# An attention and mixture-of-experts kernel: laying the attention's usual arm behind the general arm

## The chip, the core and the metric

The kernel runs on one core of one Trainium2 chip. A core has five engines that run their own instruction streams: PE (TensorE, matrix products), DVE (VectorE), ACT (ScalarE), POOL (GpSimd) and SP (SyncE, which here only issues transfers). They wait for each other by semaphores, and 16 DMA engines move data between the chip's memory and the core. The metric is the device time of one execution in microseconds (us); a time without further words is the median of several executions.

## What is computed

A windowed attention with four sink positions, and on its output a mixture of experts with one expert for each token. Cut to what matters:

```python
# attention: batch 4, heads 8, sequence 768, head size 64; n_sink = 4, window = 128
scores = q @ k.T / sqrt(64)
keep = (key < n_sink) | ((0 <= query - key) & (query - key < window))
a = softmax(where(keep, scores, -1e9))
x = (a @ v)                      # laid out as 3072 tokens x 512
# experts: 8, hidden size 1024
e = argmax(x @ w_gate); g = softmax(x @ w_gate)[e]
out = g * (relu(x @ w1[e]) @ w2[e])
```

n_sink and window are inputs of the kernel, so the kernel finds them only when it runs.

## The kernel before

The program has three stretches. In the first, to about 4 us, constants are made, the first pieces of q, k and v are loaded, and `flag()` (L711) compares n_sink and window with the usual values 4 and 128 and leaves the answer, `usual`, in a register of every engine.

The second is the attention. `tc.If(usual == 1)` (L756) has two arms. The usual arm, `fast_attention` (L448), works on tiles of 128 queries for a pair of heads, 96 steps s for 16 pairs k, and its order on each engine is written out by hand. A step holds the scores of tile s (`scores`, L509, three products of split operands f_kh, f_kl, f_qh, f_ql), the merge of masks and the maximum on DVE (L521, L523, L528), the exponentials on ACT (`exps`, L535), transposes on PE (L543), and the weighted sum with v (L570, L572). Between them ACT, DVE and POOL split the next pair's k and q into a high and a low part (`prep`: f_kh L475, f_qh L481, f_kl L478, f_ql L484), from the buffers kd and qd that SP loads (L414, L415). The loads of pairs 0 and 1 are issued ahead of the If, those of pair 2 and later, of the sinks (vs, L446) and of the gate's weights within the arm. The usual arm ends with the turn of the first tokens of expert 0 (x-rows gathered by POOL at L133, transposed at L146, split at L161 on ACT and L164 on DVE into exh and exl). The general arm, `general_attention` (L311) with the loads and splits of expert 0's weights, covers every other n_sink and window. With these inputs it isn't run. It has loops, and its instructions on every engine lie in the program's memory between the usual arm and what follows the If.

So the instructions of every engine lie in this order: the start, the compare-and-branch of the If, the usual arm, an unconditional branch past the general arm, the general arm, and the third stretch. The profile records both branches under L756.

The third stretch is the mixture of experts. It begins with the early chunk (256 tokens of expert 0, products at L911 and L933) beside the gate's last tokens (x_tp transposes at L146, gt_xT copies at L199), and with the first splits of expert 1's weights (whi on ACT at L91, wlo on DVE at L94, from wraw). Then come eight experts, each with a switch (recorded under L1114) that jumps to a body for the number of tokens the expert got.

## Time and profile before

| what | value |
|---|---|
| median of 3 executions | 628.39 us (626.49 to 630.0) |
| the profiled execution: its own time | 630.58 us |
| its span, first to last instruction | 628.9 us |
| outside the span | 1.7 us |
| mean granted share of the TensorE clock | 0.96 |
| busy: PE, PE weight loads, DVE, ACT, POOL | 89%, 77%, 49%, 44%, 35% |

Times in the profile count from the start of the span. A row of the timeline has the start, the duration, the engine, the line of the kernel, the operation, and in brackets how long the engine had been idle before it and what ended that; "issue" is idle time in which the engine waited for nothing that the profile shows. PEld is the weight load of PE; a q behind an engine's name is its sequencer, the part that reads instructions and takes branches.

### The profile page before, as it was taken

The page shows a single profiled execution, that of the slowest core. Times are in us where ns is not written, and L with a number is a line of the kernel's source. Part 1 is how long each engine was busy: PE and PEld are TensorE (multiplying, and loading weights), DVE is VectorE, ACT ScalarE, POOL GpSimd, SP SyncE. Part 2 cuts the span into 40 slices and gives each one's busy share as a digit, 9 for nine tenths or more (in the row PEclk, how much of TensorE's full clock was granted, in tenths as well). Part 3 has the DMA queues.
Part 4 walks back from the last instruction along what each step waited for, and adds up shares of the span by engine and source line. Part 5 has one row for each costly group of instructions (what it writes and reads, how often), then busy time and mean ns, then how long its engine had stood idle before and what let it go on. Part 6 is the DMA issues. An engine that isn't in the chain of part 4 may idle for free. (4 is left out here: it accounts for less than half of the span.)

```text
span 628.9 us, 11023 instructions
## 1 busy us (share of the span) xinstructions
PE 560.3 (89%) x3734; PEld 481.8 (77%) x3734; DVE 306.0 (49%) x699; ACT 274.0 (44%) x700; POOL 219.2 (35%) x384
## 2 busy tenths in 40 slices
PE   3999999799989998797979999999999978699982
PEld 2778887588767877686969988888998867598852
DVE  4676638655776476553414333453353626253300
ACT  4567665465655553522313232443343534243320
POOL 5568657573767455003014010302312111141010
PEclk9999999989998999798989999999999988899988
DMA  8234420942094106453416142463532737262010
GB/s 241 83 112 170 131 78 2 246 156 79 32 227 168 60 2 158 131 151 107 134 41 200 35 127 61 158 203 100 192 110 66 256 103 252 97 190 98 2 44 17
DMA packets 36016, 75.79 MB, mean 121 GB/s; under 512 B 4353, under 2 KB 17153, under 8 KB 35844
## 3 DMA queue, kind: packets, MB, share of 16 engines
q1 hardware_dynamic: 31204, 59.25, 31.1%
q0 software_dynamic: 4640, 14.70, 7.1%
q8 instruction: 53, 0.87, 0.6%
q14 instruction: 119, 0.97, 0.5%
HBM read 61.34 MB, written 12.99 MB: 118 GB/s over the span
## 5 line engine op out<-in xcount | busy, mean ns | idle before, releaser
L911 PE MATMUL hp<-xh,whi 128*128 128x256 f32 (+4 forms) x320 | 99.0, 309 | 16.2 <-issue 14.8
L915 ACT ACTIVATE hh<-hp 128x256 fp32r<-128x256 f32 (+4 forms) x88 | 36.0, 410 | 162.9 <-PE hp L911 162.7
L918 DVE SCALAR_TENSOR_TENSOR hl<-hp,hh 128x256 fp32r<-128x256 f32 (+4 forms) x88 | 39.7, 453 | 135.3 <-ACT hh L915 83.9
L953 POOL DMA_INDIRECT moe_out<-rows,idxs x26 | 25.4, 978 | 217.1 <-DVE rows L945 118.9
L911 PE MATMUL hp<-xh,wlo 128*128 128x256 f32 (+4 forms) x320 | 98.7, 308 | 0.0
L911 PE MATMUL hp<-xl,whi 128*128 128x256 f32 (+4 forms) x320 | 98.6, 308 | 0.0
L94 DVE TENSOR_TENSOR wlo<-wraw,whi 128x1024 fp32r<-128x1024 f32 x56 | 68.5, 1229 | 27.4 <-ACT whi L91 27.2
L911 PEld LDWEIGHTS hp<-xh,whi 128*128 128x128 f32 x320 | 64.0, 200 | 22.5 <-issue 18.7
L933 PE MATMUL yps<-whi,hh 128*128 128x512 f32 x192 | 79.3, 413 | 1.4 <-ACT hh L915 1.4
L933 PE MATMUL yps<-whi,hl 128*128 128x512 f32 x192 | 76.8, 400 | 0.0
L933 PE MATMUL yps<-wlo,hh 128*128 128x512 f32 x192 | 76.4, 398 | 0.0
L91 ACT CAST whi<-wraw 128x1024 fp32r<-128x1024 f32 (+1 forms) x72 | 68.3, 955 | 15.3 <-DMA wraw<-wcat 12.8
L535 ACT ACTIVATE f_sq<-f_sp,f_nm 128x132 f32<-128x132 f32 (+1 forms) x192 | 61.1, 374 | 27.5 <-DVE f_nm L528 27.5
L570 PE MATMUL f_po<-vt,f_pl 128*128 128x130 f32 x320 | 69.4, 298 | 0.0
L911 PEld LDWEIGHTS hp<-xl,whi 128*128 128x128 f32 x320 | 63.9, 200 | 2.5
L911 PEld LDWEIGHTS hp<-xh,wlo 128*128 128x128 f32 x320 | 63.9, 200 | 0.0
L572 PE MATMUL f_po<-vt,f_pu 128*128 128x130 f32 x320 | 63.1, 279 | 0.0
L543 PE MATMUL f_tp<-ident,f_sq 128*128 128x128 f32 x192 | 43.2, 300 | 20.6 <-ACT f_sq L535 18.4
L133 POOL DMA_INDIRECT rows<-xrow,idxg x30 | 31.8, 1061 | 80.3 <-DVE hl L918 35.6
L553 POOL TENSOR_SCALAR_AFFINE_SELECT f_pl<-f_pu 128x256 f32<-128x256 f32 x80 | 33.0, 413 | 73.9 <-ACT f_pu L547 66.6
L484 DVE SCALAR_TENSOR_TENSOR f_ql<-qd,f_qh 128x384 fp32r<-128x384 f32 x32 | 34.7, 1084 | 47.6 <-ACT f_qh L481 47.4
L570 PEld LDWEIGHTS f_po<-vt,f_pl 128*128 128x128 f32 x320 | 49.5, 194 | 7.3 <-issue 0.7
(180 smaller groups left out, 1089.5 us busy)
## 6 DMA issues: line engine op xcount, KB each, us to landing
wraw<-wcat SPq DMA_DIRECT2D x64, 512.0 KB, 4.1
xrow<-rows SPq DMA_DIRECT2D x8, 769.5 KB, 7.9
vt<-v SPq DMA_DIRECT2D x16, 384.0 KB, 4.0
kd<-kT SPq DMA_DIRECT2D x15, 396.0 KB, 5.7
qd<-qT SPq DMA_DIRECT2D x15, 384.0 KB, 9.2
rows<-xrow,idxg POOLq DMA_INDIRECT x30
moe_out<-rows,idxs POOLq DMA_INDIRECT x26
kd<-kT SPq DMA_DIRECT2D x2, 198.0 KB, 3.6
```

The source lines that it names most:

```text
L91: nc.scalar.copy(out=whi[e % 2][:, j, c], in_=wraw(e, j)[:, c])
L94: engine.tensor_tensor(out=wlo[e % 2][:, j, c], in0=wraw(e, j)[:, c], in1=whi[e % 2][:, j, c].bitcast(F32), op=ALU.subtract)
L484: V.scalar_tensor_tensor(out=ql[:, QZ[z]], in0=qd[:, QZ[z]], scalar=D ** -0.5, in1=qh[:, QZ[z]].bitcast(F32), op0=ALU.mult, op1=ALU.subtract)
L535: nc.scalar.activation(out=sqs[k][:, i, h, :n], in_=sps[u][:, h, :n], func=AF.Exp, bias=nm[:, h:h + 1], scale=1.0)
L543: nc.tensor.transpose(out=tvs[u][:, h], in_=sqs[k][:, i, h, :P], identity=ident)
L553: nc.gpsimd.affine_select(out=pl, in_=pu, pattern=[[0, 2], [1, P]], compare_op=ALU.is_ge, fill=0.0, base=0, channel_multiplier=-1)
L570: nc.tensor.matmul(out=two, lhsT=pl[:, h], rhs=twice(t), start=(i == 0 and h == 0), stop=False, skip_group_check=True)
L572: nc.tensor.matmul(out=two, lhsT=pu[:, h], rhs=twice(t - 1), start=False, stop=False, skip_group_check=True)
L911: nc.tensor.matmul(out=hp[:, :N], lhsT=l, rhs=r[:, c, :N], start=k == 0, stop=k == 3 * NK - 1)
L915: nc.scalar.activation(out=hh[:, :N], in_=hp[:, :N], func=AF.Relu)
L918: V.scalar_tensor_tensor(out=hl[:, :N], in0=hp[:, :N], scalar=0.0, in1=hh[:, :N].bitcast(F32), op0=ALU.max, op1=ALU.subtract)
L933: nc.tensor.matmul(out=y[:self.M[i]], lhsT=l[:, sl], rhs=r, start=(j == 0 and k == 0), stop=(j == NF - 1 and k == 2))
```

## The change

The If is told which of its two blocks is to lie directly behind the compare-and-branch: with `preferred_fallthrough_block=False` it is the Else block, the general arm. The usual arm lies behind the general one. Each engine now reaches the usual arm by a taken branch, and at the usual arm's end it runs on into the third stretch. No operation, no wait and no buffer is another one.

```diff
@@ -753,7 +753,7 @@
             load_qk(1, bufs)
             sink_blocks()
         usual = flag()
-        with tc.If(usual == 1) as br:
+        with tc.If(usual == 1, preferred_fallthrough_block=False) as br:
             fast_attention(bufs, vs)
         with br.Else():
             nc.sync.dma_start(out=wg, in_=w_gate)
```

## Rows read from the trace of the kernel before

**Rows 1.** The page: the span, and the busy time of each engine over it (us, share, instructions).
```profile
span 628.9 us, 11023 instructions
PE 560.3 (89%) x3734; PEld 481.8 (77%) x3734; DVE 306.0 (49%) x699; ACT 274.0 (44%) x700; POOL 219.2 (35%) x384
```

**Rows 2.** The timeline of PE, ACT and DVE around the end of the usual arm (start us, duration us, engine, line, operation, idle before and its releaser).
```profile
252.97 0.65 PE L146 MATMUL f_tp<-ident,rows 128*128 128x128 f32 x4 [0.81 <-DMA rows<-xrow,eidx]
253.66 0.59 ACT L161 CAST exh<-f_tp 128x512 fp32r<-128x512 f32 x1 [0.88 <-PE f_tp L146]
254.28 0.69 DVE L164 TENSOR_TENSOR exl<-f_tp,exh 128x512 fp32r<-128x512 f32 x1 [0.78 <-ACT exh L161]
256.56 1.09 PE L146 MATMUL x_tp<-ident,rows 128*128 128x128 f32 x4 [2.94 <-issue]
256.73 1.99 ACT L91 CAST whi<-wraw 128x1024 fp32r<-128x1024 f32 x2 [2.49 <-issue]
...
257.66 0.41 PE L911 MATMUL hp<-exl,whi 128*128 128x256 f32 x1
...
257.81 3.60 DVE L94 TENSOR_TENSOR wlo<-wraw,whi 128x1024 fp32r<-128x1024 f32 x3 [2.84 <-ACT whi L91]
```

**Rows 3.** The branches of the If at the end of the usual arm, on the sequencers of SP, PE, ACT and DVE (duration in ns three times, then first and last start in us).
```profile
L756 SPq COMPARE_BRANCH  x1: 43/43/43, 239.2 to 239.2; - x1
...
L756 PEldq COMPARE_BRANCH  x1: 3417/3417/3417, 253.0 to 253.0; - x1
L756 ACTq COMPARE_BRANCH  x1: 38/38/38, 253.7 to 253.7; - x1
L756 DVEq COMPARE_BRANCH  x1: 57/57/57, 254.3 to 254.3; - x1
```

**Rows 4.** The first instruction behind that branch on ACT, DVE and SP (semaphore instructions of L91, L94 and L88: min/median/max ns, first and last start in us, each in a stretch that begins after the branch).
```profile
L91 ACTq EVENT_SEMAPHORE  x2: 17/28/38, 256.6 to 256.7; - x2
L94 DVEq EVENT_SEMAPHORE  x3: 21/21/50, 257.3 to 258.8; - x3
L88 SPq EVENT_SEMAPHORE  x3: 17/27/28, 245.9 to 260.6; - x3
```

**Rows 5.** DMA queues that moved instructions, from 253.5 to 256 us: packets, MB, share of 16 engines.
```profile
q8 instruction: 1, 0.02, 2.6%
q14 instruction: 2, 0.02, 2.3%
```

**Rows 6.** All DMA queues after SP's branch: the first row is from 239.3 to 244.2 us (no other queue moved anything), the second is the instruction queue's from 244.2 to 244.5 us.
```profile
q1 hardware_dynamic: 483, 1.07, 105.0%
...
q14 instruction: 1, 0.01, 6.5%
```

**Rows 7.** The branches of the If at its start, on the sequencers of ACT, PE, DVE and SP (columns as in rows 3).
```profile
L756 ACTq COMPARE_BRANCH  x1: 45/45/45, 4.3 to 4.3; - x1
L756 PEldq COMPARE_BRANCH  x1: 94/94/94, 4.4 to 4.4; - x1
L756 DVEq COMPARE_BRANCH  x1: 50/50/50, 5.0 to 5.0; - x1
...
L756 SPq COMPARE_BRANCH  x1: 49/49/49, 6.5 to 6.5; - x1
```

**Rows 8.** The timeline of the usual arm's beginning, those rows that carry the argument.
```profile
4.39 0.52 ACT L475 CAST f_kh<-kd 128x396 fp32r<-128x396 f32 x1 [2.08 <-DVE highm L429]
...
6.02 0.52 ACT L475 CAST f_kh<-kd 128x396 fp32r<-128x396 f32 x1 [0.68 <-DMA kd<-kT]
...
6.55 0.52 ACT L481 ACTIVATE f_qh<-qd 128x384 fp32r<-128x384 f32 x1
...
8.63 0.43 DVE L528 TENSOR_REDUCE f_nm<-f_sp 128x2 f32<-128x256 f32 x1
...
9.60 0.52 ACT L475 CAST f_kh<-kd 128x396 fp32r<-128x396 f32 x1 [2.52 <-DMA kd<-kT]
...
10.02 0.62 ACT L535 ACTIVATE f_sq<-f_sp,f_nm 128x128 f32<-128x128 f32 x2
...
11.37 0.52 ACT L481 ACTIVATE f_qh<-qd 128x384 fp32r<-128x384 f32 x1 [0.73 <-DMA qd<-qT]
...
14.22 0.28 DVE L461 CAST vh<-vs 72x264 fp32r<-72x264 f32 x1
...
15.75 0.43 DVE L521 COPY_PREDICATED f_sp<-lowm,f_sp 128x256 f32<-128x256 uint8 x1 [1.25 <-PE f_sp L509]
...
22.46 0.53 ACT L475 CAST f_kh<-kd 128x396 fp32r<-128x396 f32 x1
```

**Rows 9.** The only DMA queue that moved anything at the start: the first row is from 4 to 6.5 us, the second from 6.5 to 16 us (packets, MB, the time that the packets took as a share of 16 engines).
```profile
q1 hardware_dynamic: 354, 0.43, 62.5%
...
q1 hardware_dynamic: 3579, 3.04, 107.8%
```

**Rows 10.** Busy time in stretches of 1 us around the end of the usual arm; the columns are the stretch and its length, the busy time of PE, PEld, DVE, ACT and POOL (instructions in brackets), the granted TensorE clock (1.00 is the level of 2.4 GHz, 0.50 that of 1.2 GHz), the DMA share and GB/s.
```profile
253.00:254.00 1.00, 0.62 (x4) 0.38 (x4) 0.50 (x1) 0.34 (x1) 0.00 (x0) 1.00 0.07 16
254.00:255.00 1.00, 0.00 (x0) 0.00 (x0) 0.69 (x1) 0.24 (x1) 0.00 (x0) 0.61 0.03 8
...
260.00:261.00 1.00, 1.00 (x6) 1.00 (x6) 0.98 (x2) 0.54 (x2) 0.00 (x0) 0.50 1.01 160
261.00:262.00 1.00, 1.00 (x11) 1.00 (x10) 0.82 (x3) 0.00 (x0) 0.00 (x0) 0.97 0.83 311
```

## The prediction

> **What bounds the kernel now.** Start with the page: PE is busy for 89% of the span and no other engine for half of it [rows 1]. So a stretch in which PE stands still for want of instructions is lost, if nothing else would have held PE there. The change touches only how the engines get into and out of the usual arm, so I read the timeline at its two ends, then the branches on the sequencers, then the queues that move instructions.

> At the arm's end three engines stop together. PE's last transposes start at 252.97 and take 0.65, ACT's last split ends at 254.25, DVE's at 254.97. Then PE does nothing until 256.56 and ACT nothing until 256.73, both for "issue": no semaphore, no transfer [rows 2]. DVE's 2.84 idle is put down to ACT, but its own sequencer is late too. The sequencers say what it is: PE's branch at 253.0 takes 3417 ns, and ACT, whose branch is at 253.7, reads its next instruction at 256.6; DVE's pair is 254.3 and 257.3 [rows 3, 4]. The same If's branch at the start, where the usual arm lies directly behind it, takes 94 ns on PE, and ACT's f_kh begins 0.09 after ACT's branch [rows 7, 8]. So the taken branch at the end costs each engine about 3 us, and in those microseconds three packets of instructions were moved [rows 5]. My reading: the target's instructions were not on the engine and had to be fetched.

> [...]

> **What the change takes away, at the arm's end.** The branches there. What is late next? ACT's whi (L91) waits only for older work (a load issued before SP's branch at 239.2, and the last write of rows), so it can follow exh at 254.2 instead of 256.73: 2.5 us. PE's x_tp transposes can follow at 253.7; the first L911 product waits for exh at 254.25, the second for exl at 254.97, so the second goes at about 255.0 to 255.1 instead of 257.66: 2.6. DVE's wlo waits for whi, which takes 1.0, and for DVE itself: 255.3 instead of 257.81, 2.5 [rows 2]. Everything behind (gate, routing, experts) hangs on these three by semaphores, and weight loads follow DVE's wlo. So the whole third stretch moves forward by **2.5 us**.

> The clock can change that. It falls from 2.4 to 1.2 GHz at about 254.4, after PE had paused several times, and is back near 261.0 [rows 10]. So PE's work from 256.5 to 261.0, 4.5 us, runs at half speed. If the clock rises at the same place of the work, nothing is added. If it never fell there, PE would gain up to 2.2 more. If it rose at the same time of day though PE starts 2.8 earlier, 2.8 more would run at half speed: 1.4 lost. Bounds of this end: a gain of 1.1 to 4.7. I take 2.5, since PE's pauses ahead of the fall stay.

> **What it adds, at the arm's start.** Every engine now takes a branch over the general arm, the same distance as at the end, so I price it by the same engines' rows. ACT's branch is at 4.3; with 2.93 its f_kh begins at 7.3, not 4.39. The cover is two transfers. In order: ACT's four splits of pair 0 begin at 0.43 apart (they no longer wait for kd, landed by 6.02), so the last f_qh begins at 8.6 instead of 6.55: 2.1 late, as 0.8 of ACT's stop fell on waits for that load. The maximum of tile 0 then ends at 11.1 instead of 9.06. The exponentials that need it began only at 10.02, because ACT stood for 2.52 until pair 1's kd landed at 9.60; they are now at 11.1, 1.1 late. Next, f_qh of pair 1 waits 0.73 for qd until 11.37; it would now begin at 11.6 or 11.7, **0.3 late**, and DVE's f_ql and the next exponentials behind it too [rows 8]. PE (4.4 and 3.4: 7.8) and DVE (5.0 and 3.0: 8.0) are back before the operand that they wait for (f_qh of pair 0, from 7.7 to 8.3) [rows 7]. The loads that make this cover are issued ahead of the If, so they don't move.

> SP's stop is longer but has more cover. At the end its branch was at 239.2 and its next instruction at 245.9, 6.7 us: until 244.2 the data queue alone filled the 16 DMA engines (105%), and the instruction packet came only behind it [rows 3, 4, 6]. At the start SP's branch is at 6.5, with the engines full from there on (107.8% from 6.5 to 16) [rows 7, 9]; I allow the same 6.7, so SP's arm begins at 13.2. Queued behind it are vs, the gate's weights, v of pair 1, kd and qd of pair 2. DVE's vh needs vs at 14.2 and has 1.25 of idle behind it; ACT needs pair 2's kd at 22.46 [rows 8]. Both should just hold.

> What if ACT's fetch is caught like SP's? When ACT branches the DMA engines are 62.5% busy (4 to 6.5), not full [rows 9]. The bounds of its stop are 2.9 (its own row) and 6.7 (SP's); the start then costs 0.3 to 4.1. I take **0.6**, near the low end, as the 62.5% lies between 2.6% and 105% but a gap before the fullness begins.

> **The sum.** 2.5 gained, 0.6 lost: 1.9 less. The profiled execution, 628.9 of span and 1.7 outside, 630.6 in all, would become 628.7; it is 2.2 above the median of the three runs, 628.4, from which I count: **626.5**.

> **The rivals.** *ACT caught behind the loads* (slower side): one mechanism, ACT's instruction packet queued behind the data of the first tiles. With the stop at 6.7 instead of 2.9 the start costs 4.1 and the sum is 628.4 - 2.5 + 4.1 = 630.0. It decides from a stop of 5.1 us on, where start and end are even; for a loss of over 3.1 us the stop would have to be 8.2. For it: SP's row at 244.2. Against it: ACT branches 2 us before the engines fill up. 15%, a third of it as slow as over 631.5.

> *The clock gives more*: PE's pause of 2.9 gone, the low stretch shrinks or vanishes: 2.2 more at most: 628.4 - 2.5 - 2.2 + 0.6 = 624.3. For it: PE works without a break from 253.7. Against it: the clock was already falling while PE's transposes had just ended. 20%.

> *Nothing moves*: the layout isn't as told, or running on at the arm's end needs a fetch just as long, since the next piece of program is not there yet. Against it: PE, busy for 89% of the span, runs through nearly all of its 3734 products in order, and can't lose 3 us often by it [rows 1]; and the untaken branch at the start cost 0.09. 628.4, 10%.

> **How the numbers follow.** The forecast itself has 55%: 626.5, its own range 625.3 to 628.0. Three runs of before lie between 626.49 and 630.0, so a difference under some 0.5%, 3.1 us, can't be told from none. Faster than 625.3: most of the clock's 20%, and a tenth of the forecast's: 0.25. Slower than 631.5: 0.06, ACT caught for 8 us, or SP's late loads holding DVE as well. The same: 0.69. The range, 624.0 to 629.3, takes in the clock's case and the lower half of the case of ACT caught, and leaves out the tails.

> **What would show it.** In the changed kernel PE's branch at the start takes about 3.4 us and none stands at the arm's end; f_kh begins near 7.3 and the exponentials of tile 0 near 11.1; instruction packets appear at 5 to 6 us, SP's vs near 13; at the end x_tp follows the last exh transposes within 0.2, and from there to the last instruction the trace is as long as before. It is wrong if f_kh begins past 9, if vs or kd of pair 2 stops DVE or ACT, or if PE still waits for "issue" behind the last transposes of the arm.

## The result

The changed kernel takes 631.8 us, the median of 19 executions (629.54 to 634.96), beside 628.39 for 19 of the kernel before on the same chip (624.87 to 631.35). The ratio is 1.0056, with a 95% interval of 1.0037 to 1.0075: slower by about 3.5 us. The forecast was 626.5 with a range of 624.0 to 629.3, so it was wrong, in sign too.

The page of the profile after answers to [rows 1]. Nothing there has moved: what was lost is too small for the page.

```profile
span 629.8 us, 11018 instructions
PE 560.0 (89%) x3734; PEld 480.9 (76%) x3734; DVE 305.5 (49%) x699; ACT 273.9 (43%) x700; POOL 218.8 (35%) x384
```

The branches of the If, all of them now at the start, answer to [rows 3] and [rows 7] (duration in ns three times, first and last start in us).

```profile
L756 ACTq COMPARE_BRANCH  x1: 50/50/50, 4.3 to 4.3; - x1
L756 PEldq COMPARE_BRANCH  x1: 3892/3892/3892, 4.4 to 4.4; - x1
L756 DVEq COMPARE_BRANCH  x1: 67/67/67, 4.9 to 4.9; - x1
L756 POOLq COMPARE_BRANCH  x1: 50/50/50, 5.2 to 5.2; - x1
L756 SPq COMPARE_BRANCH  x1: 50/50/50, 8.1 to 8.1; - x1
```

The timeline of the usual arm's beginning answers to [rows 8].

```profile
4.75 0.52 ACT L475 CAST f_kh<-kd 128x396 fp32r<-128x396 f32 x1 [2.44 <-DVE highm L429]
...
8.31 0.47 PE L509 MATMUL f_sp<-f_kh,f_qh 64*128 64x128 f32 x2 [8.31 <-issue]
...
12.91 1.03 DVE L484 SCALAR_TENSOR_TENSOR f_ql<-qd,f_qh 128x384 fp32r<-128x384 f32 x2 [8.52 <-issue]
...
13.52 0.47 PE L509 MATMUL f_sp<-f_kh,f_ql 64*128 64x128 f32 x2 [4.74 <-DVE f_ql L484]
...
14.78 0.42 DVE L528 TENSOR_REDUCE f_nm<-f_sp 128x2 f32<-128x256 f32 x1
...
15.30 0.63 ACT L535 ACTIVATE f_sq<-f_sp,f_nm 128x128 f32<-128x128 f32 x2 [4.12 <-DVE f_nm L528]
...
15.81 0.52 ACT L481 ACTIVATE f_qh<-qd 128x384 fp32r<-128x384 f32 x1
```

Beside it, the same f_ql in the kernel before:

```profile
5.37 0.56 DVE L484 SCALAR_TENSOR_TENSOR f_ql<-qd,f_qh 128x384 fp32r<-128x384 f32 x1 [0.97 <-ACT f_qh L481]
```

Read the rows after the change from the bottom. Tile 0's exponentials start at 15.30 instead of 10.02. They wait for the maximum, that for PE's products, those for f_ql, and f_ql for nothing but "issue". Pair 1's f_qh is 4.44 late (15.81 for 11.37), and this lateness stays through the attention: the last exh starts at 258.32 instead of 253.66 [rows 2], 4.66 late. (That it stays so exactly is this pair of traces. In the 17 profiled runs of this document, from tile 0's exponentials to the last exh it is 240.1 to 244.3 us, so one trace carries such an account to some 2 us, and the medians carry the rest.)

DVE's own queue shows that this was not one long stop. The row is DVE's semaphore waits recorded under L484 up to 13.2 us.

```profile
L484 DVEq EVENT_SEMAPHORE  x2: 21/21/21, 9.3 to 12.9; - x2
```

The first of the two is the usual arm's first instruction on DVE, a wait for q of pair 0. It ran at 9.3, 4.4 us after the branch. The second instruction, f_ql, ran only at 12.91. Between the two DVE stood for another 3.6 us, and all of its operands were long there.

At the arm's end the stop is gone; this answers to [rows 2].

```profile
257.63 0.66 PE L146 MATMUL f_tp<-ident,rows 128*128 128x128 f32 x4 [0.78 <-DMA rows<-xrow,eidx]
258.12 0.82 PE L146 MATMUL x_tp<-ident,rows 128*128 128x128 f32 x4
258.32 0.59 ACT L161 CAST exh<-f_tp 128x512 fp32r<-128x512 f32 x1 [0.85 <-PE f_tp L146]
258.81 2.00 ACT L91 CAST whi<-wraw 128x1024 fp32r<-128x1024 f32 x2
...
259.69 0.58 PE L911 MATMUL hp<-exl,whi 128*128 128x256 f32 x1
259.89 1.22 DVE L94 TENSOR_TENSOR wlo<-wraw,whi 128x1024 fp32r<-128x1024 f32 x1 [0.25 <-ACT whi L91]
```

exl's product is 2.03 late and wlo 2.08, against 4.66 ahead of it: 2.6 us came back here, as in every profiled run without a stop at the arm's end: from the last exh to exl's product it is 4.00 before, and 1.36 or 1.37 in all of them. Some was given back again, since the clock fell all the same. The stretches answer to [rows 10].

```profile
257.00:258.00 1.00, 0.37 (x3) 0.37 (x4) 0.49 (x1) 0.47 (x1) 0.00 (x0) 1.00 0.03 8
258.00:259.00 1.00, 0.98 (x8) 0.58 (x6) 0.25 (x2) 0.68 (x2) 0.00 (x0) 0.68 0.00 0
...
264.00:265.00 1.00, 1.00 (x7) 1.00 (x6) 0.17 (x1) 0.00 (x0) 0.00 (x0) 0.50 0.78 303
265.00:266.00 1.00, 1.00 (x9) 0.98 (x9) 0.00 (x0) 1.00 (x2) 0.00 (x0) 0.91 0.87 324
```

PE now works at a granted clock of 0.50 from 258.4 to 265.2, where before it worked so from 256.5 to 261.0 (the views give the clock as a share of full speed, 1.00 and 0.50; no run shows it in GHz): 2.2 us more at half speed (there is a short idle piece in 259 to 260), 1.1 lost. So: 4.7 lost at the start, 2.6 gained at the end, 1.1 lost to the clock, 3.2 in all; the ratio says 3.5. The two profiled spans differ by 0.9 only: the profiled execution of before was 2.2 above its median, that of after, 631.5, is at its own. So of the 3.2 by which the two traces differ at 265 us, 2.3 are gone by the end. No row here explains that; the changed kernel's own two traces differ there by as much (370.1 and 372.5 us from exl's product to the end).

### The profile page after: what moved, and what is told of

It reads as the page before. It is cut to its first block, busy times and chain, and to the rows that moved or that the text cites. A ratio compares the mean times of both kernels' runs of the same rounds, so it can differ in the third digit from the quotient of the medians.

```text
span 629.8 us, 11018 instructions
## 1 busy us (share of the span) xinstructions
PE 560.0 (89%) x3734; PEld 480.9 (76%) x3734; DVE 305.5 (49%) x699; ACT 273.9 (43%) x700; POOL 218.8 (35%) x384
## 5 line engine op out<-in xcount | busy, mean ns | idle before, releaser
L911 PE MATMUL hp<-xh,whi 128*128 128x256 f32 (+4 forms) x320 | 98.0, 306 | 13.6 <-issue 12.5
L911 PE MATMUL hp<-xl,whi 128*128 128x256 f32 (+4 forms) x320 | 97.6, 305 | 0.0
L911 PE MATMUL hp<-xh,wlo 128*128 128x256 f32 (+4 forms) x320 | 97.4, 304 | 0.0
L94 DVE TENSOR_TENSOR wlo<-wraw,whi 128x1024 fp32r<-128x1024 f32 x56 | 68.2, 1224 | 24.4 <-ACT whi L91 24.3
L911 PEld LDWEIGHTS hp<-xh,whi 128*128 128x128 f32 x320 | 62.9, 197 | 20.1 <-issue 16.2
L91 ACT CAST whi<-wraw 128x1024 fp32r<-128x1024 f32 (+1 forms) x72 | 68.3, 955 | 12.3 <-DMA wraw<-wcat 12.3
L911 PEld LDWEIGHTS hp<-xl,whi 128*128 128x128 f32 x320 | 63.1, 197 | 2.5
L911 PEld LDWEIGHTS hp<-xh,wlo 128*128 128x128 f32 x320 | 62.9, 197 | 0.0
L484 DVE SCALAR_TENSOR_TENSOR f_ql<-qd,f_qh 128x384 fp32r<-128x384 f32 x32 | 34.4, 1077 | 53.7 <-ACT f_qh L481 45.2
L133 POOL DMA_INDIRECT rows<-xrow,idxg x30 | 33.4, 1115 | 76.9 <-DVE hl L918 33.7
```

Source lines behind the costliest of these rows:

```text
L91: nc.scalar.copy(out=whi[e % 2][:, j, c], in_=wraw(e, j)[:, c])
L94: engine.tensor_tensor(out=wlo[e % 2][:, j, c], in0=wraw(e, j)[:, c], in1=whi[e % 2][:, j, c].bitcast(F32), op=ALU.subtract)
L133: nc.gpsimd.indirect_dma_start(out=rows[q][:, i], out_offset=None, in_=xrow[:n], in_offset=bass.IndirectOffsetOnAxis(ap=icol, axis=0))
L484: V.scalar_tensor_tensor(out=ql[:, QZ[z]], in0=qd[:, QZ[z]], scalar=D ** -0.5, in1=qh[:, QZ[z]].bitcast(F32), op0=ALU.mult, op1=ALU.subtract)
L911: nc.tensor.matmul(out=hp[:, :N], lhsT=l, rhs=r[:, c, :N], start=k == 0, stop=k == 3 * NK - 1)
```

## The experiments

In the tables of this section "first" is when the usual arm's first instruction ran on DVE (us), and ratios are to executions of the kernel before on the same chip beside them, with their 95% intervals.

### Hints for the branch: is it one fetch caught behind the loads?

The first theory (T) was that DVE's one fetch is queued behind the loads issued ahead of the If. A branch hint, the call in the diff with the branch's name and "LikelyTaken", stands at the start of the program and was to bring the fetch forward. With hints on all engines the trace has one BRANCH_PREFETCH_HINT on each, 45 to 58 ns long, at 0.8 to 0.9 us.

```diff
+        tc.mark_branch_hint_location("att", "LikelyTaken", engines=[mybir.EngineType.PE, mybir.EngineType.Activation, mybir.EngineType.DVE, mybir.EngineType.SP, mybir.EngineType.Pool])
         with tc.manual_schedule(engines={mybir.EngineType.SP}):
...
-        with tc.If(usual == 1, preferred_fallthrough_block=False) as br:
+        with tc.If(usual == 1, preferred_fallthrough_block=False, label="att") as br:
```

All engines:

> The changed kernel, and at the program's very start every engine is told which branch will be taken (a branch hint for the If), so that the usual arm's first instructions can be fetched before the first loads fill the DMA engines. Theory T (DVE's stop from its branch at 4.9 to 12.91 us is a fetch queued behind the loads, and this stop is what made the change slower): DVE's first f_ql comes near 5.4 us as before, the exponentials of tile 0 at 10.0 to 10.4 instead of 15.30, nothing stops at the arm's end, and the time is 1.0 to 2.7 us below the kernel before (ratio 0.9957 to 0.9985). Rival 1 (a branch over the general arm costs DVE 8 us however early its target is known): f_ql near 12.9, ratio 1.004 to 1.008. Rival 3 (the start is not the reason, the time is lost behind the attention by the clock): f_ql near 5.4, but the ratio stays above 1.003.

DVE alone:

> As the changed kernel, with the branch hint for DVE alone. PE, ACT, POOL and SP branch as in the changed kernel. T: f_ql near 5.4; PE comes back at 8.3 and SP near 12.0 as in the changed kernel; from PE's return to the exponentials of tile 0 it is 1.8 to 2.1 us and pair 1's kd lands by 10.7, so they start at 10.4 to 11.3; ratio 0.996 to 1.000. Rival 2 (SP's late loads or PE's stop set the delay): the exponentials of tile 0 or the tiles of pairs 1 and 2 stay 4 us late though f_ql is early, ratio above 1.003.

All but DVE:

> As the changed kernel, with the branch hint for PE, ACT, POOL and SP, but not for DVE. T: PE and SP run on without a stop, DVE's f_ql still comes only at 11 to 13 us, the exponentials of tile 0 at 13.5 to 15.3, ratio 1.002 to 1.008 as in the changed kernel. Rival 2 (PE's or SP's stop): ratio 0.996 to 0.999.

| run | first | f_ql | exponentials of tile 0 | ratio |
|---|---|---|---|---|
| all engines | 9.0 | 9.06 | 11.46 | 0.9949 (0.9927 to 0.9971) |
| DVE alone | 9.1 | 9.20 | 11.59 | 0.994 (0.9908 to 0.9972) |
| all but DVE | 9.7 | 9.76 | 12.15 | 0.9975 (0.9951 to 0.9999) |

The hints did not do what they were meant to: with hints on all engines PE's branch still took 4064 ns, DVE still stopped for 4 us, and the data's queue was the only one that moved anything from 0.5 to 4.4 us. Yet the gap between DVE's first two instructions was gone in all three, also where DVE had no hint. T fell: where DVE had no hint, its stop was 4.6 us, not 8. What differs is that second gap of 3.6 us.

### The end by itself

```diff
         with br.Else():
             nc.sync.dma_start(out=wg, in_=w_gate)
-            general_attention()
-            for j in range(AHEAD):
-                load_weights(0, j)
-            for j in range(NF):
-                split_weights(0, j)
```

This is made from the kernel before (its usual arm first), not from the changed one.

> The kernel before, its general arm cut down to the load of the gate's weights; with these inputs that arm is not run, so nothing that runs is left out. The usual arm lies first as before, and at its end every engine branches, but over a few instructions only. It shows the end's share by itself, with the start as before. T (the 3 us at the end are a fetch of instructions that lie far ahead): PE's branch at the end takes under 0.3 us instead of 3417 ns, x_tp follows the last transposes within 0.3, and the time is 1.0 to 2.7 us below the kernel before (ratio 0.9957 to 0.9985). Rival (an unconditional branch costs 3 us whatever the distance): PE's branch still takes 3.4 us, ratio 0.999 to 1.001. If the clock gives all of it back: the stop is gone, and the ratio is 0.999 to 1.001 all the same.

Measured: 0.995 (0.9922 to 0.9978), a little below the expected 0.9957 to 0.9985. The branches of PE, the one at the start and the one at the end, and the timeline at the end:

```profile
L756 PEldq COMPARE_BRANCH  x2: 94/139/184, 4.4 to 252.1; - x2
```

```profile
252.09 0.66 PE L146 MATMUL f_tp<-ident,rows 128*128 128x128 f32 x4 [0.69 <-DMA rows<-xrow,eidx]
252.58 0.60 PE L146 MATMUL x_tp<-ident,rows 128*128 128x128 f32 x4
...
253.38 2.00 ACT L91 CAST whi<-wraw 128x1024 fp32r<-128x1024 f32 x2
```

The branch at the end takes 184 ns over a few instructions and 3417 over the general arm [rows 3]. So the end's 3 us come with the far target, and by the three packets that moved in them [rows 5] I read them as its fetch. Taking them away was worth about 3 us here, with the clock, which did not fall. That price was measured once, in the same set of runs as the three hints, whose ratios came out higher when they were run again (below).

### The place of the arm's first instruction

The second theory (T2): DVE's usual arm begins in the last place of an instruction packet (8192 bytes: in the kernel before, 119 packets on q14 moved 0.97 MB), and the next packet comes late. Writes on DVE in the general arm, which isn't run, move the usual arm along without running anything.

```diff
         with br.Else():
             nc.sync.dma_start(out=wg, in_=w_gate)
+            for _ in range(5):        # 64, 132, 126 in the others
+                V.memset(least, -BIG)
             general_attention()
```

The first run is the changed kernel as it is.

> The changed kernel once more, beside its variants. What the runs before showed: with a hint on any engines DVE's first instruction of the usual arm (a semaphore wait) comes at 9.0 to 9.7 us and f_ql 0.08 behind it; in the changed kernel that first instruction came at 9.34 too, but f_ql, the second one, only at 12.91. Theory T2: DVE's usual arm begins with the last instruction that one instruction packet (8192 bytes) holds, so DVE needs two packets, and the second is queued behind the loads; in the changed kernel the two moved at 7.37 and 11.04. Theory T1 as before: the 8 us are one fetch caught behind the loads, and which execution catches it is chance. T2 expects the gap again between DVE's first and second instruction of the arm (f_ql at 10 to 13), and a ratio of 1.003 to 1.008. T1 expects that the first instruction itself may come late or early, and that a second look differs at will.

Four instructions more (five writes; one separate wait falls away):

> As the changed kernel, with a few small writes on DVE added to the general arm, which with these inputs is not run: nothing else is executed, but DVE's usual arm lies four instructions further on. T2: its first instructions now lie together in one packet, so f_ql follows DVE's first instruction within 0.2 us, at 8.9 to 9.8 us, the exponentials of tile 0 start at 11.3 to 12.2 instead of 15.30, and the ratio is 0.993 to 0.998. T1 (one fetch, by chance): as the changed kernel, ratio 1.003 to 1.008, or no system between the two.

Sixty:

> The same with 60 instructions more on DVE in the general arm that is not run. T2: as with four (f_ql at 8.9 to 9.8, ratio 0.993 to 0.998), since only the place within the packet matters and not the distance of the jump. A rival by which the distance of the jump counts: f_ql not earlier than with four, and ratio between that run and the changed kernel.

128:

> As the changed kernel, with 128 instructions more on DVE in the general arm that is not run. An instruction packet of 8192 bytes moves 128 instructions if one takes 64 bytes, so T2 (the place within the packet decides) puts the usual arm's first instruction back into the last place of a packet: the gap returns, DVE's first instruction at 9.0 to 9.8, f_ql 2.3 to 4.2 us behind it, the exponentials of tile 0 at 14 to 16, ratio 1.002 to 1.008. If the four and the sixty instructions more had helped for another reason (the longer jump, chance), f_ql follows the first instruction within 0.2 us and the ratio is 0.994 to 1.000.

122:

> The same with 122 instructions more: by T2 seven instructions of the usual arm lie in the first packet, both f_ql of pair 0, tile 0's merge and its maximum among them, and the gap comes behind the maximum. T2: f_ql at 9.0 to 9.8, the exponentials of tile 0 at 11.3 to 12.3, and then DVE's eighth instruction only at 11.5 to 13.8 (it waits for pair 1's q until 11.5 anyway), so pair 1 is 0 to 2 us later than with four instructions more; ratio 0.994 to 1.003. If the place doesn't matter, it is as with four more at every point.

In the next one the 64 writes stand on POOL instead, and so does the write of least at L430. It is this write by which DVE's program is one instruction shorter, and not a wait, as the expectation has it.

```diff
-        V.memset(least, -BIG)
+        nc.gpsimd.memset(least, -BIG)
...
+            for _ in range(64):
+                nc.gpsimd.memset(least, -BIG)
             general_attention()
```

> As the changed kernel, with 63 small writes more on POOL in the general arm that is not run; DVE's program is one instruction shorter by it (a wait has moved to POOL), so DVE's usual arm begins in the last place but one. T2, if DVE's packets are counted from the start of its own program: DVE's first instruction and the first f_ql come together at 9.0 to 9.8, and the gap of 2.3 to 4.2 us comes before the third instruction; the exponentials of tile 0 at 13 to 16, ratio 1.001 to 1.008. If the packets are cut elsewhere (by where the programs of all engines lie in memory), the gap can be gone, with a ratio of 0.994 to 1.000.

| instructions more on DVE | first | next after the gap | gap from the first | exponentials of tile 0 | ratio |
|---|---|---|---|---|---|
| 0 (19 executions above) | 9.3 | 2nd, 12.91 | 3.6 | 15.30 | 1.0056 (1.0037 to 1.0075) |
| 0, again | 9.5 | 2nd, 13.49 | 4.0 | 15.88 | 1.0048 (1.0028 to 1.0068) |
| 128 | 9.2 | 2nd, 12.70 | 3.5 | 15.10 | 1.0074 (1.0044 to 1.0104) |
| -1 | 9.1 | 3rd, 12.7 | 3.6 | 14.24 | 1.0041 (1.0016 to 1.0066) |
| 122 | 9.3 | 8th, 12.8, with its data | not shown | 12.11 | 0.9982 (0.9955 to 1.001) |
| 4 | 9.2 | none | | 11.88 | 0.9985 (0.9963 to 1.0006) |
| 60 | 9.2 | none | | 11.71 | 0.9992 (0.9961 to 1.0023) |

The rows behind it, DVE's semaphore waits under L484 and its f_ql. With 128 more:

```profile
L484 DVEq EVENT_SEMAPHORE  x2: 21/21/21, 9.2 to 12.7; - x2
12.70 1.03 DVE L484 SCALAR_TENSOR_TENSOR f_ql<-qd,f_qh 128x384 fp32r<-128x384 f32 x2 [8.30 <-issue]
```

With one fewer:

```profile
9.19 0.56 DVE L484 SCALAR_TENSOR_TENSOR f_ql<-qd,f_qh 128x384 fp32r<-128x384 f32 x1 [4.77 <-issue]
12.72 0.56 DVE L484 SCALAR_TENSOR_TENSOR f_ql<-qd,f_qh 128x384 fp32r<-128x384 f32 x1 [2.97 <-issue]
```

With 122 more (the last of the three waits is the arm's eighth instruction):

```profile
L484 DVEq EVENT_SEMAPHORE  x3: 21/21/21, 9.3 to 12.8; - x3
9.36 1.03 DVE L484 SCALAR_TENSOR_TENSOR f_ql<-qd,f_qh 128x384 fp32r<-128x384 f32 x2 [4.95 <-issue]
12.11 0.62 ACT L535 ACTIVATE f_sq<-f_sp,f_nm 128x128 f32<-128x128 f32 x2
```

With four more:

```profile
9.30 1.03 DVE L484 SCALAR_TENSOR_TENSOR f_ql<-qd,f_qh 128x384 fp32r<-128x384 f32 x2 [4.90 <-issue]
11.88 0.62 ACT L535 ACTIVATE f_sq<-f_sp,f_nm 128x128 f32<-128x128 f32 x2
```

T2 holds for the runs of this section. 128 instructions on, the gap returns in the same place; with one fewer it moves one instruction back; with four and sixty more there is none (their ratios, expected from 0.993 to 0.998, are just above that). With 122 more T2 puts it ahead of the eighth instruction, behind the maximum of tile 0. The first seven indeed run without a gap, but the eighth waits for pair 1's q, whose last piece landed at 12.75 us in this trace, 0.06 ahead of it; with four more the same instruction ran at 12.61, 0.03 behind its q. So this run shows that nothing is lost there, not that the gap is there. (The runs with hints on all but DVE don't fit; see the end of this part.)

In the four runs with the gap the instruction behind the cut runs 3.5 to 4.0 us after the arm's first one. The packets show when the next one moves. In the kernel before, at the arm's end, PE, ACT and DVE ran their first instructions at 256.56, 256.6 and 257.3 [rows 2, 4]; from 256.5 to 258 us only these moved, at 257.06 (q8), 257.22 and 257.90 (q14):

```profile
q8 instruction: 1, 0.02, 5.9%
q14 instruction: 2, 0.02, 3.6%
```

### What the loads have to do with it

```diff
+                load_v(0, bufs)
+                load_qk(1, bufs)
                 ops, prep_of = {}, {}
...
-            load_v(0, bufs)
-            load_qk(1, bufs)
             sink_blocks()
```

The two calls move from ahead of the If to the first operations of the usual arm.

> As the changed kernel, but the loads of v of pair 0 and of k and q of pair 1 are issued as the first operations of the usual arm instead of ahead of the If. DVE's arm still begins in the last place of a packet. SP then branches at about 4.6 and fetches on idle DMA engines. Both theories: DVE's two packets move before 7.5, f_ql at 7.9 to 9.0. SP comes back at 7.5 to 8.5 and issues the loads then, 3 to 4 us later than in the kernel before; pair 1's k lands at 12.5 to 14, and the exponentials of tile 0, which stand behind its split, start at 13 to 14.5. So ratio 0.998 to 1.006. If f_ql still comes near 12.9, the loads are not what holds the packets.

Measured: 1.0045 (1.0022 to 1.0069). DVE's waits, its f_ql, and all DMA queues from 6.8 to 8.7 and from 8.7 to 9.8 us:

```profile
L484 DVEq EVENT_SEMAPHORE  x2: 21/21/21, 8.7 to 11.1; - x2
11.08 1.03 DVE L484 SCALAR_TENSOR_TENSOR f_ql<-qd,f_qh 128x384 fp32r<-128x384 f32 x2 [6.69 <-issue]
```

```profile
q8 instruction: 1, 0.02, 3.1%
...
q14 instruction: 2, 0.02, 4.9%
```

I had expected f_ql by 9.0, and missed. No data moved from 5.7 to 10.1 us. DVE's first stop is 3.8 us here, not 4.4, and the gap behind its first instruction 2.4, not 3.6. The packets tell the same as above: PE, SP and DVE ran their first instructions at 8.03, 8.67 and 8.73, and the next packets moved at 8.69 (q8), 9.23 and 9.29 (q14, by the order above the queue of engines other than PE), 0.56 to 0.66 behind. So the loads lengthen the two stops by 0.6 and 1.2 us, as far as one trace tells; the most of both, 6.2 us, is there with hardly any data on the way. SP, which had only the first pieces of q and k to issue ahead of its branch, came back only at 8.67, and pair 1's k was late by it (its f_kh at 13.48), so the ratio is no better.

### Do hints help by themselves?

The kernels without the gap lay between 0.994 and 0.9992, so three were run beside each other: the hint on DVE alone, the four instructions more, and hints on all engines together with the 64 writes on DVE. The one with hints on all but DVE was run again too.

> The changed kernel with the hint on DVE alone, once more, beside the kernel with four instructions more on DVE in the general arm. If a hint does nothing but take a place in DVE's program (which moves the usual arm's first instruction out of the last place of its packet), both have the same start (f_ql at 9.0 to 9.4) and ratios that can't be told apart, 0.994 to 0.999, by the sum 2.5 to 2.7 gained at the end, 0.6 to 1.2 lost at the start. If the hint helps by itself, f_ql or the instruction packets come earlier here, and its ratio is lower by 0.3% or more.

> The changed kernel with four instructions more on DVE in the general arm, once more, in the same call as the kernel with the hint. f_ql at 9.0 to 9.8; ratio 0.994 to 0.999; by the rival that the hint counts by itself, 0.998 to 1.000.

> Hints on all engines and sixty instructions more on DVE in the general arm. If only the place counts: as the other two, f_ql at 9.0 to 9.8, ratio 0.994 to 0.999. If hints count: the lowest of the three.

> The run with hints on PE, ACT, POOL and SP once more. DVE's program is instruction for instruction that of the changed kernel, yet in the first run f_ql followed DVE's first instruction by 0.08 us at 9.76. If that was chance (both packets happened to come together), the gap is back here, f_ql at 11 to 13.5. If the place of DVE's program differs by the hints of the other engines, there is again no gap, f_ql at 9.0 to 9.9, ratio 0.994 to 0.999.

| run | f_ql | exponentials of tile 0 | ratio |
|---|---|---|---|
| hint on DVE alone, again | 9.51 | 11.90 | 0.9985 (0.9957 to 1.0014) |
| four instructions more, again | 9.41 | 11.80 | 0.9991 (0.9967 to 1.0016) |
| hints and sixty more | 9.57 | 11.96 | 1.0002 (0.9974 to 1.0029) |
| hints on all but DVE, again | 9.24 | 11.71 | 1.0008 (0.9977 to 1.0039) |

No effect of a hint by itself is seen; on DVE it takes a place in the program (the one hint at 0.8 us), which by T2 is enough. The ten runs without the gap ahead of tile 0's merge have a mean ratio of 0.9981, 1.2 us below the kernel before; the five with it have 1.0053, 3.3 above. Those of the first set were measurably faster than the kernel before, the same kernel or its like later was not: the seven later runs of the ten are 0.5 us below it. So none is shown to beat it, and the last two of the table lie above the 0.994 to 0.999 expected. All ten ratios lie below the changed kernel's interval.

Open: with hints on all but DVE, DVE's instructions are those of the changed kernel one for one, and the gap was absent twice. Counted in DVE's own program alone, the cut would be where it is in the changed kernel. Perhaps it depends on another engine's program too, though not on POOL's, where 64 writes more moved nothing; no run tests that. So that the place in the packet decides is shown; what sets the place is not shown in full.

## Why the prediction was wrong

**What failed: the stop on DVE.** The step was "PE (4.4 and 3.4: 7.8) and DVE (5.0 and 3.0: 8.0) are back before the operand that they wait for". DVE's first instruction ran at 9.3 and its second at 12.91. Two things were missed. The first fetch is 4.4 us here and not 3.0, even 3.8 without loads; the row at the arm's end was no price for it. And a branch's target can need two packets one behind the other: I priced one. With one packet the loss would have been small: with four instructions more f_ql is at 9.30, and the exponentials, forecast for 11.1, start at 11.88. Nor was there the cover argued for PE and DVE. It was ACT's late f_qh of pair 0, forecast to end at 8.3; it ended at 5.70, so that PE and DVE themselves, back at 8.31 and 9.34, set when tile 0 began.

**The slower rival had the wrong engine.** It put ACT's packet behind the loads, at 15%, and the chance left for slower by over 0.5% was 0.06. ACT hardly stopped: f_kh is at 4.75, 0.36 late, not at 7.3. POOL's f_kl was as little late. So "every engine now takes a branch over the general arm, the same distance as at the end" was wrong by engine: ACT and POOL went on after 0.5 us, PE, DVE and SP after 3.9 to 4.4. That the targets of ACT and POOL were on these engines already would fit; no run shows it. None of the prediction's own signs of being wrong came: they watch f_kh, SP's loads and the arm's end, and none of them DVE's first two instructions.

**What held.** PE's branch at the start took 3892 ns (forecast: about 3.4 us) and PE was back at 8.31. SP went on at 12.03 (allowed: 13.2), and its late loads stopped nothing; but that is two errors against each other, since its branch came at 8.1 and not at 6.5, and its stop was 3.9 and not 6.7. The end gave 2.6 (forecast 2.5), with x_tp right behind the last transposes. "Nothing moves" is refuted by that end. "The loads that make this cover ... don't move" held only in part: pair 1's k came some 1 us later (f_kh at 10.65 for 9.60; in the other runs with the taken branch at the start and the loads ahead of it, 10.4 to 11.7).

**The clock.** The bound of a loss of 1.4, "if it rose at the same time of day", has nearly the size of the measured 1.1, but not by its mechanism: the clock fell 4 us later and rose 4 us later. That the pause ahead of it is what makes the clock fall can't be held: it fell at the arm's end in the changed kernel's two profiles (0.68 from 258 to 259 us, 0.78 from 255 to 260), with four more on DVE it didn't (1.00 from 250 to 270), with 122 more it did (0.51 from 255 to 260), each time without the pause. What decides it stays open. (In the kernel before it fell at 254.2, not at 254.4; nothing hangs on that.)

**The sum** without the gap was 1.9 gained; the ten runs have 1.2, the seven later ones 0.5. The end's term held (2.6 for 2.5). The start's was mis-sized even without the gap: pair 1's f_qh, which it had 0.3 late, is 0.6 to 1.4 late in the ten runs (11.97 to 12.77 for 11.37). The term that was left out turned the sign: 4.5 us, the difference of the two means, or 3.8 within the two sets that have runs of both kinds. The traces show 3.4 of it at tile 0.

## What to carry to other kernels

In these runs a taken branch to far code cost PE, DVE and, at the arm's end, ACT a stop of 2.9 to 4.6 us, SP 3.5 to 6.7, and DVE a second one of 2.4 to 4 when its target was in the last place or two of a packet. Four instructions more on DVE, or one fewer, were enough to remove or move that second one. Before moving such a branch, ask engine by engine how much work it has behind the target's first instructions and who waits for it, and place it where the engine on the critical chain has some. When two kernels that run the same instructions differ by a few microseconds, look for an engine idle for "issue" with its operands there, then at its own queue's first two instructions.

## What was not expected of the hardware

The next instruction packet behind a taken branch moved only when the first instruction of the target had run, 0.5 to 0.7 us later with little data on the way (the kernel before at the arm's end, and the run with the loads moved), and what lay in it ran 3.5 to 4.0 us after that first instruction (2.4 with the loads moved away). Hints on all engines at 0.8 us, some 4 us ahead of the branches, moved no packet earlier: up to 5.8 us there was none, and in the changed kernel the first moved at 5.4. And POOL and ACT were over their general arm within 0.5 us (branches at 5.2 and 4.3, going on at 5.7 and 4.75), 0.4 more than an untaken branch cost them.
